# A gated mix of linear attention and a Fourier transform: the hidden transform as seven products of quarters in place of four half products

## The chip, the cores and the metric

The kernel runs on one core of one Trainium2 chip. The metric is the device time of one execution in microseconds (us), the median of several runs; less is better. The core has engines that work side by side, each on its own queue of instructions in order: TensorE (PE, matmuls), VectorE (DVE), ScalarE (ACT), GpSimd (POOL), and SyncE (SP), which here issues most DMA transfers between DRAM and the on-chip memory. They wait for each other by semaphores. Results of matmuls go to eight banks of an accumulator memory.

## The reference

What is computed, cut to its core (S = 2048, D = 576, H = 32 heads of 18 columns, all in 32-bit floats):

```python
q, k, v = qkv[0], qkv[1], qkv[2]             # from x @ wqkv
phi = lambda t: jnp.where(t > 0, t + 1, jnp.exp(t)) + 1e-6
kv = jnp.einsum("bhsd,bhse->bhde", phi(k), v)
a  = num / den @ wo                          # linear attention with phi(q), kv
re = jnp.einsum("bsd,ed->bse", x, dft_hid_re)
im = jnp.einsum("bsd,ed->bse", x, dft_hid_im)
y  = jnp.einsum("ts,bse->bte", dft_seq_re, re) - jnp.einsum("ts,bse->bte", dft_seq_im, im)
g  = sigmoid((x * gate_w).sum(-1, keepdims=True))
out = g * a + (1 - g) * y
```

## The kernel before, in words

Matmuls take operands of a reduced format that keeps the upper bits of a float. Each operand is therefore split: its high part is a copy into that format (`hi_of`, L111, on ScalarE), its low part the rest (`lo_of`, L114, on VectorE), and a full product is three matmuls: high by high, high by low, low by high. Sums ahead of a split are VectorE's (`add`, L117).

S is cut into 16 row tiles of 128, D into four tiles of 128 and a last one of 64, the columns into two halves of 288. The stages, in order:

- K: 16 tiles of x, 28 matmuls each (`k_half`, L266), give phi(k).
- Products over S (L399 to L413, 448 matmuls), from which the per-head matrices come.
- Q: 16 tiles, then products with a matrix M that folds kv and wo into one. Its result, scaled by the gate, is kept in 16 tiles `acc`.
- For the real and then the imaginary part of the transform: a **hidden stage** (`pairs`, L531 to L606) and a **sequence stage** (`sequence`, L645).

The hidden stage takes row tiles in eight pairs (p, p+8). A pair is four products, two tiles by two column halves, of 14 matmuls each (L123): 56. From the four results, VectorE and ScalarE make seven combined factors and split them (`columns` and `rest`). The sequence stage is a product of the 2048x2048 transform with these factors in seven products of quarters instead of eight. It has 32 steps (eight row tiles j of four blocks b); a step uses one matrix block `c` (high and low part) in 42 matmuls (L663). `Matrix.load` (L620) brings a block's 512 KB as `craw`, `Matrix.make` (L629) sums (one 128x512 step and two 128x256), then splits it into two 128x1792 parts. Step n loads block n+3 and makes block n+2. At the end of a row tile, `mix` (L676) adds the result, weighted by the gate, to `acc`; the second sequence stage stores `acc` as the output.

Blocks of `craw` and `c`, the weights and the tiles of x share seven slots of the on-chip memory, laid out by the tables LAY_R and LAY_I. So a block can be loaded only once the reader of what lay there is done. Pairs are counted from 0 to 7. In the program, block 0 is loaded and made after pair 4, block 1 within pairs 6 and 7.

SP's queue follows the program's order up to `in_order.close()` (L759). The order on the other engines, and on SP behind that line, is made by a scheduler that simulates the program. GpSimd has no transfers; it builds masks at the start.

## Time and profile before

| what | us |
|---|---|
| median of 3 runs (lowest, highest) | 745.35 (744.57, 745.51) |
| the profiled execution | 745.01 |
| its span | 743.3 |
| hidden stages in that span, from first to last matmul | 264.43 to 323.79, 502.22 to 561.56 |

In the page, a line such as `L663 PE MATMUL bank<-f,c ... x2688 | 356.9, 295 | 0.0` gives a source line, the engine, the operation, what it writes and reads, the count, the busy time, the mean of one in ns (matmuls overlap, so the mean is longer than the distance of their starts), and the idle time ahead. A row of the timeline gives start, length, engine, line and count, and in brackets the idle time ahead with what ended it. Names in such rows are tiles: `craw` a matrix block as it is summed, `c` its split parts, `f` the factors, `tsum` and `y` the sums at the end of a pair or row tile, `xs` the split tiles of x, `wd` the split weights.

### The profile page before, as it was taken

Reading aid. Unit: us, or ns where it says so; the run is one execution under the profiler, and the core shown is the slowest. Engines: PE = TensorE matmul, PEld = TensorE weight load, DVE = VectorE, ACT = ScalarE, POOL = GpSimd, SP = SyncE. Lnnn points to the kernel's source line nnn. Section 1 sums busy time; section 2 is a strip of 40 time slices with the busy share of each in tenths; the row PEclk is TensorE's granted clock in tenths of the full one; section 3 lists DMA queues with packets and bytes.
Section 4 is the critical chain, followed back from the end, with each engine's and each line's share of the span. In section 5 each row is a group of like instructions: output and inputs, shape, how many; then the busy total and the mean of one; then the engine's idle time right before and its main releaser. Section 6 shows DMA issues by size and latency. Waiting matters only on the chain.

```text
span 743.3 us, 13515 instructions
## 1 busy us (share of the span) xinstructions
PE 735.4 (99%) x5540; PEld 734.1 (99%) x5540; DVE 543.2 (73%) x917; ACT 331.9 (45%) x536; POOL 1.6 (0%) x10
## 2 busy tenths in 40 slices
...
GB/s 168 90 90 158 179 106 145 54 169 72 36 59 92 1 82 89 72 86 115 114 86 88 112 86 86 114 118 117 90 77 113 67 159 130 117 125 139 117 118 33
DMA packets 31715, 75.55 MB, mean 102 GB/s; under 512 B 3301, under 2 KB 9061, under 8 KB 31653
## 3 DMA queue, kind: packets, MB, share of 16 engines
...
q10 hardware_dynamic: 288, 0.41, 0.2%
q14 instruction: 19, 0.15, 0.1%
...
## 4 chain that ended last, share of the span: by engine, by line
PE 99%; DMA 0%; DVE 0%; issue 0%; ACTq 0%; ACT 0%; DVEq 0%
PE bank L663 48%; PE bank L123 41%; PE bank L408 8%; PE bank L719 1%; DMA xraw<-in_xa_dram 0%; PE bank L391 0%; PE bank L394 0%; DVE acc L679 0%; DVE wd L115 0%; DVE xs L285 0%; ACTq L225 0%; ACT L147 0%; DVEq L115 0%; DVE xs L115 0%
## 5 line engine op out<-in xcount | busy, mean ns | idle before, releaser
L663 PE MATMUL bank<-f,c 128*128 128x288 f32 x2688 | 356.9, 295 | 0.0
L663 PEld LDWEIGHTS bank<-f,c 128*128 128x128 f32 x2688 | 356.6, 188 | 0.1
L123 PE MATMUL bank<-wd,xs 128*128 128x288 f32 (+1 forms) x1792 | 243.7, 297 | 4.5 <-DVE xs L115 3.8
L123 PEld LDWEIGHTS bank<-wd,xs 128*128 128x128 f32 x1792 | 240.7, 190 | 5.4 <-ACT wd L112 4.4
L112 ACT ACTIVATE c<-craw 128x1792 fp32r<-128x1792 f32 (+1 forms) x84 | 121.3, 1448 | 225.2 <-DVE craw L118 184.4
L115 DVE TENSOR_TENSOR c<-craw,c 128x1792 fp32r<-128x1792 f32 (+2 forms) x84 | 141.7, 1690 | 37.9 <-ACT c L112 37.7
L118 DVE TENSOR_TENSOR craw<-craw 128x256 f32<-128x256 f32 (+1 forms) x192 | 96.4, 509 | 50.4 <-DMA craw<-in_cr_dram 24.7
L115 DVE TENSOR_TENSOR xs<-xraw,xs 128x640 fp32r<-128x640 f32 (+1 forms) x65 | 52.5, 809 | 17.0 <-ACT xs L112 16.7
L123 PE MATMUL bank<-mw,qs 128*128 128x288 f32 x448 | 63.3, 297 | 0.0
L408 PE MATMUL bank<-pk,c 128*128 128x288 f32 x448 | 60.9, 296 | 0.0
L123 PEld LDWEIGHTS bank<-mw,qs 128*128 128x128 f32 x448 | 60.0, 188 | 0.0
L112 ACT ACTIVATE xs<-xraw 128x640 fp32r<-128x640 f32 x63 | 46.3, 737 | 30.4 <-DMA xraw<-in_xa_dram 30.1
L408 PEld LDWEIGHTS bank<-pk,c 128*128 128x128 f32 x448 | 59.8, 188 | 0.0
L118 DVE TENSOR_TENSOR y<-bank,y 128x288 f32<-128x288 f32 x63 | 28.6, 454 | 10.0 <-PE bank L663 9.3
L258 DVE SCALAR_TENSOR_TENSOR acc<-bank,e 128x288 f32<-128x288 f32 x64 | 27.8, 450 | 10.8 <-ACT e L257 10.7
L256 ACT ACTIVATE e<-bank 128x288 f32<-128x288 f32 x64 | 25.6, 401 | 19.2 <-PE bank L123 19.2
L115 DVE TENSOR_TENSOR f<-tsum,f 128x1152 fp32r<-128x1152 f32 x16 | 21.7, 1356 | 13.3 <-ACT f L112 13.3
L257 ACT ACTIVATE e<-e 128x288 f32<-128x288 f32 x64 | 28.0, 439 | 1.0
L112 ACT ACTIVATE f<-bank 128x288 fp32r<-128x288 f32 x48 | 19.2, 402 | 19.6 <-PE bank L123 11.0
L738 ACT ACTIVATE acc<-bank,gate 128x288 f32<-128x288 f32 x32 | 16.0, 500 | 26.4 <-PE bank L123 26.2
L115 DVE TENSOR_TENSOR f<-bank,f 128x288 fp32r<-128x288 f32 x48 | 21.4, 448 | 8.6 <-ACT f L112 8.6
L112 ACT ACTIVATE f<-tsum 128x1152 fp32r<-128x1152 f32 x16 | 18.6, 1162 | 17.3 <-DVE tsum L118 17.3
...
## 6 DMA issues: line engine op xcount, KB each, us to landing
...
```

What stands on the lines that cost most here:

```text
L112: return nc.scalar.activation(dst, src, AF.Copy, bias=bias)
L115: nc.vector.tensor_tensor(out=dst, in0=src, in1=hi, op=ALU.subtract)
L118: nc.vector.tensor_tensor(out=dst, in0=a, in1=b, op=op)
L123: nc.tensor.matmul(ps, a, b, start=(n == 0), stop=(n == len(pairs) - 1))
L256: nc.scalar.activation(e, ps, AF.Relu, scale=-1.0)
L257: nc.scalar.activation(e, e, AF.Exp, scale=-1.0)
L258: nc.vector.scalar_tensor_tensor(dst, ps, 0.0, e, op0=ALU.max, op1=ALU.add)
L408: nc.tensor.matmul(ps[h][:, :HALF], t[:, a, k], pk[s][:, b, half(h)], start=(s == 0 and n == 0), stop=(s == NT - 1 and n == len(passes) - 1))
L663: nc.tensor.matmul(ps[q], c[x][:, l, k], factors[p][:, y, f], start=(p == 0 and i == 0), stop=(p == NP - 1 and i == 2))
L719: nc.tensor.transpose(banks[c // KC][:, (c % KC) * P:(c % KC + 1) * P], a, ident)
L738: nc.scalar.activation(acc[i][:, half(h)], ps[:, :HALF], AF.Copy, scale=gate[:, i:i + 1])
```

## The change

Over D, x and the hidden weights are cut into quarters: the two halves of D by the two tiles of a pair, and the halves of D by the two column halves. Each half of D has 288 = 2 x 128 + 32 rows. A pair's products become seven products of combined quarters. Each is six matmuls (two tiles of 128 rows, three passes) and one of 96 rows, which holds the three passes of the 32-row rest: 49 matmuls a pair. Results are accumulated in four banks, and the seven factors are sums of them, on VectorE (seven 128x288 sums, a 128x288 split and a 128x1728 split for a pair).

The combined forms are made ahead and kept in DRAM. `Left` makes the forms of x in nine blocks during K and the products over S: a load by GpSimd, four sums of 128x256, a split (128x1792 on both engines), and a store of 1.8 MB by GpSimd. `right` makes the weights' forms in three pieces for each of the two weights, in the Q stage and in the first sequence. The class `Hidden` loads them: seven forms of weights for a stage, seven of x for each pair (262 KB each, into buffers for two pairs: x(p+2,k) follows product k of pair p), and the rest rows (three transfers a pair, runs of 512 bytes). For this, `acc` is no longer kept: GpSimd stores it to DRAM in the Q stage, `sequence` loads its rows as `row` tiles, the first sequence stores the mixed rows as `mid`, and the second loads these. Block 0 is now loaded in pair 6 and made in pair 7; blocks 1 and 2 are loaded in pair 7, and block 1 is made there.

```diff
+PRODUCTS = {1: (4, 0), 6: (2, 4), 2: (6, 1), 5: (1, 3), 7: (0, 5), 3: (3, 2), 4: (5, 6)}
+ORDER = (3, 2, 7, 6, 1, 4, 5)
...
+class Layout:
+    def __init__(self, swap):
+        self.swap = swap
+        a, b = (2, 0) if swap else (0, 2)
+        slot = [SLOT_AT + k * SLOT for k in range(7)]
+        self.low = [slot[a + 1 - swap], WF_AT] + [slot[k] for k in (b + 1 - swap, 4, 6, a + 1 - swap)]
+        self.high = [slot[a + swap], WF_AT + 2 * WF] + [slot[k] for k in (b + swap, 5, a + swap)]
+    def x(self, p, k):
+        h = (p + self.swap) % 2
+        return SLOT_AT + h * 7 * XF + (k if self.swap else 6 - k) * XF
+    def rest(self, p):
+        return WF_AT + 4 * WF if p % 2 else SLOT_AT + 14 * XF + 3 * WF
+    def w(self, k):
+        return WF_AT + k * WF if k < 4 else SLOT_AT + 14 * XF + (6 - k) * WF
...
+    class Left:
+        def __init__(self, k, start, after):
+            self.c = at(start, [P, 7, 2, 2 * P], R, "xb")
+            self.f = self.c.bitcast(F)
+            self.k = k
+            begin_after(nc.gpsimd.dma_start(out=self.f[:, 3:7, 1], in_=xq[k]), after)
+        def make(self):
+            r, c = self.f[:, :, 1], self.c
+            add(r[:, 0], r[:, 4], r[:, 3], ALU.subtract)
+            add(r[:, 1], r[:, 5], r[:, 3])
+            add(r[:, 2], r[:, 1], r[:, 4], ALU.subtract)
+            add(r[:, 3], r[:, 6], r[:, 2], ALU.subtract)
+            hi_of(c[:, :, 0], r)
+            lo_of(c[:, :, 1], r, c[:, :, 0])
+            nc.gpsimd.dma_start(out=xforms[self.k], in_=self.f)
+    def right(src, rest, start):
+        main, last = scratch([P, 7, 2, 2, HALF], "wm"), scratch([96, 7, HALF], "wm")
+        def pieces():
+            for k in range(3):
+                n = P if k < 2 else 96
+                c = at(start, [P, 7, 2, HALF], R, "wb")[:n]
+                f = c.bitcast(F)
+                r = f[:, :, 1]
+                if k < 2:
+                    nc.gpsimd.dma_start(out=r[:, 0:3], in_=src[k, :, 0:3])
+                    nc.gpsimd.dma_start(out=r[:, 5], in_=src[k, :, 3])
+                else:
+                    for j in range(3):
+                        rows = slice(32 * j, 32 * j + 32)
+                        nc.gpsimd.dma_start(out=r[rows, 0:3], in_=rest[:, 0:3])
+                        nc.gpsimd.dma_start(out=r[rows, 5], in_=rest[:, 3])
+                yield
+                add(r[:, 3], r[:, 5], r[:, 0], ALU.subtract)
+                add(r[:, 5], r[:, 2], r[:, 5], ALU.subtract)
+                add(r[:, 4], r[:, 2], r[:, 3], ALU.subtract)
+                add(r[:, 6], r[:, 4], r[:, 1], ALU.subtract)
+                hi_of(c[:, :, 0], r)
+                if k < 2:
+                    lo_of(c[:, :, 1], r, c[:, :, 0])
+                    nc.gpsimd.dma_start(out=main[:, :, k], in_=f)
...
+        if i % 3 == 2 and i // 3 < 4:
+            left = Left(i // 3, SLOT_AT + 15104 + i // 3 % 2 * 14336, done[-1])
+        if i % 3 == 1:
+            left.make()
...
-            if step in (4, 5):
-                wqt.load(step - 4)
-            if step >= 8:
+            for k, (a, o) in enumerate(((0, SLOT_AT + 15104), (3, SLOT_AT + 29440), (6, ACC_AT),
+                                        (10, ACC_AT), (13, ACC_AT + 14336))):
+                if step == a:
+                    left = Left(4 + k, o, done[-1])
+                if step == a + 2:
+                    left.make()
+            if step in (8, 9):
+                wqt.load(step - 8)
+            if step >= 11:
...
+        if i in (5, 7, 9):
+            next(wr_pieces, None)
...
-            if p == NP - 4:
-                m.load(0)
-                m.make(0)
...
+    class Hidden:
+        def __init__(self, weights, lay):
+            (self.main, self.last), self.lay = weights, lay
+            self.w, self.x, self.rest = {}, {}, {}
+        def load_w(self, k):
+            f, o = PRODUCTS[ORDER[k]][1], self.lay.w(k)
+            wl, rl = at(o, [P, 4, HALF], R, "wf"), at(o + 4 * HALF * 4, [P, HALF], R, "wf")
+            wm, rm = wl.bitcast(F), rl.bitcast(F)
+            nc.sync.dma_start(out=wm.rearrange("p (c s) n -> p c s n", c=2), in_=self.main[:, f])
+            nc.sync.dma_start(out=rm[:96], in_=self.last[:, f])
+            self.w[k] = wl, rl
+        def load_rest(self, p):
+            g, row = p // 4, p % 4 * 32
+            self.rest[p] = at(self.lay.rest(p), [P, 7, P], R, "xr")
+            r = self.rest[p].bitcast(F)
+            for j in range(3):
+                nc.sync.dma_start(out=r[32 * j:32 * j + 32],
+                                  in_=xforms[NP][row:row + 32, :, j // 2, g * P:g * P + P])
+        def load_x(self, p, k):
+            o = self.lay.x(p, k)
+            self.x[p, k] = at(o, [P, 4, P], R, "xf")
+            r = self.x[p, k].bitcast(F)
+            nc.sync.dma_start(out=r.rearrange("p (s c) n -> p s (c n)", s=2),
+                              in_=xforms[p][:, PRODUCTS[ORDER[k]][0]])
+        def product(self, ps, p, k, start):
+            x, (w, wl) = self.x[p, k], self.w[k]
+            ops = [(x[:, a * 2 + c], w[:, 2 * c + b]) for c in range(2) for a, b in FULL]
+            ops.append((self.rest[p][:96, PRODUCTS[ORDER[k]][0]], wl[:96]))
+            for n, (a, b) in enumerate(ops):
+                nc.tensor.matmul(ps, a, b, start=(start and n == 0), stop=(n == len(ops) - 1),
+                                 skip_group_check=True)
+        def run(self, m):
+            for p in range(NP):
+                hi = at(T_AT + p * TPAIR, [P, 7, HALF], R, "fh")
+                o = T_AT + p * TPAIR + 7 * HALF * 4
+                t, lo = (at(o, [P, 7, HALF], d, "fl") for d in (F, R))
+                p3, p2, e = (at(y_ring.next(), [P, HALF], F, "y") for _ in range(3))
+                be, bx, bg, bf = (bank()[:, :HALF] for _ in range(4))
+                for k, q in enumerate(ORDER):
+                    ps = {3: be, 6: be, 5: be, 2: bx, 1: bx, 7: bg, 4: bf}[q]
+                    self.product(ps, p, k, q in (3, 2, 7, 4))
+                    if p + 2 < NP:
+                        self.load_x(p + 2, k)
+                    if p == NP - 2 and k == 3:
+                        m.load(0)
+                    if p == NP - 1 and k == 0:
+                        m.make(0)
+                    if p == NP - 1 and k == 1:
+                        m.load(1)
+                    if p == NP - 1 and k == 4:
+                        m.load(2)
+                        m.make(1)
+                    if q == 3:
+                        nc.scalar.activation(p3, be, AF.Copy)
+                    elif q == 2:
+                        nc.scalar.activation(p2, bx, AF.Copy)
+                    elif q == 7:
+                        add(t[:, 5], bg, p3, ALU.subtract)
+                    elif q == 6:
+                        add(e, be, p2, ALU.subtract)
+                    elif q == 1:
+                        hi_of(hi[:, 0], bx)
+                        add(t[:, 4], bx, t[:, 5])
+                        lo_of(lo[:, 0], bx, hi[:, 0])
+                    elif q == 4:
+                        add(t[:, 6], bf, e, ALU.subtract)
+                        add(t[:, 1], t[:, 4], t[:, 6], ALU.subtract)
+                    else:
+                        add(t[:, 3], be, p2, ALU.subtract)
+                        add(t[:, 2], t[:, 3], t[:, 4])
+                if p + 2 < NP:
+                    self.load_rest(p + 2)
+                hi_of(hi[:, 1:], t[:, 1:])
+                lo_of(lo[:, 1:], t[:, 1:], hi[:, 1:])
+                factors.append((hi, lo))
...
-                o = self.low.next()
+                n, low = self.loaded, self.lay.low
+                o = low[n] if n < 2 else low[2 + (n - 2) % 4]
...
+                row = {t: at(mix_ring.next(), [P, D], F, "row") for t in (j, j + NP)}
+                for t, a in row.items():
+                    nc.sync.dma_start(out=a, in_=src[t])
...
+                    nc.sync.dma_start(out=dst[t][:, cs], in_=a)
...
+        nc.gpsimd.dma_start(out=att[i], in_=acc[i])
+        if i == 1:
+            next(wr_pieces, None)
+        if 6 <= i < 9:
+            hidden.load_w(i - 2)
+        if i >= 9:
+            hidden.load_x(0, i - 9)
+            hidden.load_x(1, i - 9)
+        for k, j in enumerate((9, 10, 12, 14)):
+            if i == j:
+                hidden.load_w(k)
+        if i == 10:
+            hidden.load_rest(0)
+    hidden.load_rest(1)
...
     def late(n):
+        if n in (4, 8, 12, 16):
+            next(wi_pieces, None)
+        if n == 20:
+            for k in range(4):
+                second.load_w(k)
         if n == NP * NB - 3:
+            second.load_rest(0)
+            for k in range(3):
+                second.load_x(0, k)
         if n == NP * NB - 2:
-    pairs(wdr, mr)
-    sequence(mr, gate_n, between=late)
+            for k in range(3, 7):
+                second.load_x(0, k)
+            second.load_w(4)
+        if n == NP * NB - 1:
+            second.load_w(5)
+            second.load_w(6)
+            second.load_rest(1)
+            for k in range(7):
+                second.load_x(1, k)
+    first.run(mr)
+    sequence(mr, gate_n, att, mid, between=late)
     factors.clear()
-    pairs(wdi, mi)
-    sequence(mi, gate_m, last=gate_n)
+    second.run(mi)
+    sequence(mi, gate_m, mid, [out[t * P:(t + 1) * P] for t in range(NT)], last=gate_n)
```

**VectorE at the first handover.** Before, block 0 (`craw_3754`, `c_3760`) stands among the steps of the first pair; `f` and `tsum` are that pair's factors:

```order
L115 TENSOR_TENSOR f_3399<-bank,f_3399 128x288
L118 TENSOR_TENSOR craw_3754<-craw_3754 128x512
L118 TENSOR_TENSOR craw_3754<-craw_3754 128x256 x2
L115 TENSOR_TENSOR f_3399<-bank,f_3399 128x288
L115 TENSOR_TENSOR c_3760<-craw_3754,c_3759 128x1792
L118 TENSOR_TENSOR tsum_3404<-tsum_3404,bank 128x288
L118 TENSOR_TENSOR tsum_3404<-bank,tsum_3404 128x288
L115 TENSOR_TENSOR xs_3375<-xraw_3376,xs_3375 128x640
```

After, these rows stand at the end of the stage. `craw_4115`, `craw_4180`, `craw_4206` and `craw_4300` are blocks 0, 1, 2 and 4, `c_4169` is the low part of block 0, `fl_4076` the wide split of pair 6, `fl_4149` and `fl_4150` are steps of pair 7, of which the last before `c_4169` needs the last hidden product; ahead of the first row stands the 128x512 sum of `craw_4180`:

```order
L159 TENSOR_TENSOR craw_4115<-craw_4115 128x256
L159 TENSOR_TENSOR fl_4149<-bank,fl_4149 128x288
L159 TENSOR_TENSOR craw_4206<-craw_4206 128x512
L159 TENSOR_TENSOR craw_4180<-craw_4180 128x256
L156 TENSOR_TENSOR fl_4150<-bank,fh_4148 128x288
L156 TENSOR_TENSOR fl_4076<-fl_4075,fh_4074 128x1728
L159 TENSOR_TENSOR craw_4300<-craw_4300 128x512
L159 TENSOR_TENSOR craw_4206<-craw_4206 128x256
L159 TENSOR_TENSOR craw_4180<-craw_4180 128x256
L159 TENSOR_TENSOR fl_4149<-bank,y_4153 128x288
L159 TENSOR_TENSOR fl_4149<-bank,y_4152 128x288
L156 TENSOR_TENSOR c_4169<-craw_4115,c_4168 128x1792
```

The low part of block 0 has moved from the first pair to a place behind the sums of blocks 1, 2 and 4 and the steps of pair 7.

**TensorE at the same place.** Before, the last product of a pair is followed by the sequence with both parts of block 0 (`c_3759` high, `c_3760` low):

```order
L123 MATMUL bank<-wd_2876,xs_3848 128x288 x2
L123 MATMUL bank<-wd_2877,xs_3848 128x288
L123 MATMUL bank<-wd_2876,xs_3848 128x288 x3
L663 MATMUL bank<-f_3399,c_3759 128x288 x2
L663 MATMUL bank<-f_3399,c_3760 128x288
L663 MATMUL bank<-f_3484,c_3759 128x288 x2
L663 MATMUL bank<-f_3484,c_3760 128x288
```

After, the end of pair 7 (`xf_40..` its forms, `xr_4068` its rest rows, `wf_..` the weights' forms and, one number on, their rest) and the start of the sequence, with `fh` and `fl` the factors' parts and `c_4168` the high part of block 0:

```order
L697 MATMUL bank<-wf_3193,xr_4068 128x288
L697 MATMUL bank<-wf_3249,xr_4068 128x288
L697 MATMUL bank<-wf_3361,xr_4068 128x288
L697 MATMUL bank<-wf_3074,xr_4068 128x288
L697 MATMUL bank<-wf_3468,xf_4031 128x288 x6
L697 MATMUL bank<-wf_3469,xr_4068 128x288
L697 MATMUL bank<-wf_3021,xf_4041 128x288 x6
L697 MATMUL bank<-wf_3022,xr_4068 128x288
L697 MATMUL bank<-wf_3136,xf_4064 128x288 x6
L697 MATMUL bank<-wf_3137,xr_4068 128x288
L803 MATMUL bank<-fh_3534,c_4168 128x288
L803 MATMUL bank<-fl_3536,c_4168 128x288
```

The rest products of pair 7 with the first four forms stand apart from their main products, and the first 14 matmuls of the sequence use the high part alone; the low part `c_4169` follows in the 15th.

**GpSimd in the K stage.** Before, its queue has no transfers. After, its queue holds the loads of `Left` (`xb`) and the stores of the forms (`xm`):

```order
L317 DMA xb_312<-in_xq_dram 128x4x256
L327 DMA xm_94<-xb_312 128x3584
L317 DMA xb_456<-in_xq_dram 128x4x256
L317 DMA xb_600<-in_xq_dram 128x4x256
L327 DMA xm_95<-xb_456 128x3584
L327 DMA xm_96<-xb_600 128x3584
L317 DMA xb_744<-in_xq_dram 128x4x256
L317 DMA xb_992<-in_xq_dram 128x4x256
L327 DMA xm_97<-xb_744 128x3584
L317 DMA xb_1096<-in_xq_dram 128x4x256
L327 DMA xm_98<-xb_992 128x3584
```

A store waits for the split of its block, and the loads behind it stand in the same queue.

182 lines of the change are left out of this document (74 added, 108 removed).

## The prediction

> **What bounds the kernel now.** I began with the first and fourth parts of the page and the list of what TensorE waits for.
>
> ```profile
> span 743.3 us, 13515 instructions
> PE 735.4 (99%) x5540; PEld 734.1 (99%) x5540; DVE 543.2 (73%) x917; ACT 331.9 (45%) x536; POOL 1.6 (0%) x10
> DMA packets 31715, 75.55 MB, mean 102 GB/s; under 512 B 3301, under 2 KB 9061, under 8 KB 31653
> PE 99%; DMA 0%; DVE 0%; issue 0%; ACTq 0%; ACT 0%; DVEq 0%
> PE bank L663 48%; PE bank L123 41%; PE bank L408 8%; PE bank L719 1%; DMA xraw<-in_xa_dram 0%; PE bank L391 0%; PE bank L394 0%; DVE acc L679 0%; DVE wd L115 0%; DVE xs L285 0%; ACTq L225 0%; ACT L147 0%; DVEq L115 0%; DVE xs L115 0%
> ```
> ```profile
> PE bank L123 <- DVE xs L115: 3.8, 1, 3.8
> PE bank L123 <- DVE wd L115: 0.4, 1, 0.4
> PE bank L123 <- DVE xs L285: 0.2, 1, 0.2
> ```
>
> The reader sees a kernel that is a row of matmuls and nothing else: TensorE is busy for 99% of the span, the chain of waits is TensorE from end to end, and all its waits together are 4.4 us, at the start. So a matmul removed is time removed, as long as no new wait appears. Every wait that the change makes is paid in full, since no idle time of TensorE is there to take it.
>
> Next came the stages. The windows view, cut at the first matmuls of each stage (start to end, length, then busy time and count of each engine), and the timeline of TensorE at the two places where a hidden stage hands over to a sequence stage (start, length, instructions):
>
> ```profile
> 264.43:323.79 59.36, 59.36 (x450) 59.36 (x449) 41.32 (x76) 29.58 (x51) 0.00 (x0) 1.00 0.29 85
> 323.79:502.22 178.43, 178.43 (x1347) 178.29 (x1345) 142.11 (x202) 62.07 (x50) 0.00 (x0) 1.00 0.31 101
> 502.22:561.56 59.34, 59.34 (x451) 59.34 (x450) 45.93 (x83) 30.12 (x52) 0.00 (x0) 1.00 0.31 94
> ```
> ```profile
> 323.79 28.40 PE L663 MATMUL bank<-f,c 128*128 128x288 f32 x212
> ...
> 561.56 8.63 PE L663 MATMUL bank<-f,c 128*128 128x288 f32 x64
> ```
>
> Each hidden stage is 448 matmuls in 59.36 and 59.34 us, 0.1325 us each, at a granted clock of 1.00. Neither handover has an idle bracket: the sequence starts at once. The next rows say why. They are VectorE's at 269 us, some 50 us ahead of the first sequence matmul:
>
> ```profile
> 269.02 1.61 DVE L118 TENSOR_TENSOR craw<-craw 128x512 f32<-128x512 f32 x3 [1.63 <-DMA craw<-in_cr_dram]
> ...
> 272.45 2.02 DVE L115 TENSOR_TENSOR c<-craw,c 128x1792 fp32r<-128x1792 f32 x1 [1.45 <-ACT c L112]
> 274.39 0.45 DVE L118 TENSOR_TENSOR tsum<-tsum,bank 128x288 f32<-128x288 f32 x1
> ```
>
> The first matrix block is loaded, summed and split early in the stage, so nothing is due at its end.
>
> **The gain.** Seven matmuls for eight on the same 128x288 shape: 56 to 49 a pair, 8 pairs, two stages, 112 removed, 112 x 0.1325 = 14.84 us. The seven rest matmuls of a pair have 96 rows instead of 128; I take them at the same price, since the columns that stream are the same.
>
> **The first handover.** The change loads block 0 in pair 6 and makes it in pair 7, and loads blocks 1 to 4 as the stage's buffers come free. The price of this is VectorE's queue at the end of the stage, which the order above shows. Its steps are priced from these rows (the spacing of starts is what a queued step costs):
>
> ```profile
> L115 DVE TENSOR_TENSOR c<-craw,c 128x1792 fp32r<-128x1792 f32 x64 | 129.1, 2020 | 15.5 <-ACT c L112 15.5
> ```
> ```profile
> 368.61 0.33 SPq L625 DMA_DIRECT2D craw<-in_cr_dram  x1
> ...
> 369.18 0.44 DVE L118 TENSOR_TENSOR y<-y,bank 128x288 f32<-128x288 f32 x1
> 369.54 0.41 DVE L118 TENSOR_TENSOR craw<-craw 128x256 f32<-128x256 f32 x1
> 369.88 0.45 DVE L118 TENSOR_TENSOR y<-bank,y 128x288 f32<-128x288 f32 x1
> ...
> 371.86 0.69 DVE L118 TENSOR_TENSOR craw<-craw 128x512 f32<-128x512 f32 x1 [0.47 <-DMA craw<-in_cr_dram]
> 372.47 0.45 DVE L118 TENSOR_TENSOR y<-bank,y 128x288 f32<-128x288 f32 x1
> ```
>
> A 128x288 step costs 0.36 us, 128x256 0.34, 128x512 0.61, and 128x1792 1.94 (272.45 to 274.39); 128x1728 is then 1.87. A block's load takes 371.86 - 368.61 = 3.25 us from issue to the step that waited for it.
>
> Let E be the end of the last hidden matmul. By the new order of TensorE, block 1's buffer (the first two weight forms) has its last reader 23 matmuls before E, at E-3.05, so it lands at E+0.2; block 2 is issued behind it, and with 0.5 MB at the 385 GB/s quoted below it lands 1.4 us later, at E+1.6; block 4's buffer (under the form of the fifth product) is free at E-1.86. VectorE, in order, from E+0.2: block 1's first sum 0.61, 0.34, a step of pair 7 0.36, to E+1.5; block 2's from its landing, 0.61, 0.34, 0.36, to E+2.9; the wide split of pair 6 1.87, E+4.8; block 4's sum 0.61, then 0.34, 0.34, 0.36, 0.36, E+6.8; at last the low part of block 0, 1.94, E+8.8. TensorE has 14 sequence matmuls that use block 0's high part only, 1.86 us. It then waits 8.8 - 1.86 = 6.9 us, taken as **7.0**. Lower end: all blocks have landed in time, and and only the steps behind pair 7's fifth product (E-1.86) count: 0.36+0.61+0.34+0.36+1.87+0.61+0.34+0.34+0.36+0.36+1.94 = 7.5, so E+5.6 and a wait of 3.8. Upper end: loads collide with pair loads and land 2.5 us later, 9.5.
>
> **The second handover.** The same queue, with other neighbours. Block 1's buffer is free 30 matmuls before E, lands at E-0.7, and the low part of block 0 stands behind ten steps: 0.61+0.34+0.36+0.36+0.36+0.61+0.34+0.36+0.61+0.34 and 1.94 are 6.2, so E+5.5 and a wait of 3.7 us as the lower end. One of the ten frees the bank into which pair 7's last product accumulates, and with it that product waits as well, inside the same 3.7. Blocks 2 and 4 land up to 1.5 us late as before, 0.8 taken, and the low part of block 1 comes about 7 us after block 0's, where one step of the sequence (42 x 0.1325 = 5.6 us) gives less cover: 1.5 us more. I take **6.0**, from 3.7 to 8.
>
> **Between first sequence and second hidden stage.** Four quarters of pair 1 and two weight forms lie under the last sequence buffers and can only be issued once these are read: 2.3 MB, 0.33 us an issue, 3.25 us to land. The sixth product of pair 0 is due 35 matmuls (4.6 us) after the start. I take **1.5 us**, between 0 (all in time) and 6 (the forms land last at 385 GB/s).
>
> **The hidden stages' transfers.** A pair needs 7 x 262 KB and 344 KB of rest rows, 2.18 MB in 6.49 us, 336 GB/s, where before moved 85 (row above). What the trace has at its busiest, by windows (last three numbers: clock, share of the DMA engines, GB/s):
>
> ```profile
> 3.00:9.00 6.00, 4.53 (x15) 3.68 (x16) 4.57 (x11) 3.60 (x8) 0.00 (x0) 1.00 1.01 356
> 62.00:66.00 4.00, 4.00 (x32) 4.00 (x32) 2.55 (x4) 2.49 (x7) 0.00 (x0) 1.00 0.96 319
> 86.00:91.00 5.00, 5.00 (x42) 5.00 (x41) 4.42 (x7) 2.00 (x4) 0.00 (x0) 1.00 1.00 324
> 221.00:226.00 5.00, 5.00 (x40) 5.00 (x40) 4.09 (x13) 3.77 (x9) 0.00 (x0) 1.00 1.06 385
> ```
>
> Six pairs are loaded within a stage, 13.1 MB: 41 us at 319 GB/s, due at about 51. Buffers for two pairs hide that. The second stage has 2.3 MB more, 48 us at 319. So nothing is late by itself, but little is spare: **1.0 us** for both, from 0 to 5 (280 GB/s, 55 us in the second).
>
> **K, S and Q stages.** Here VectorE and ScalarE also prepare the forms: nine blocks of x, each 4 x 0.34 + 1.94 = 3.3 us of VectorE and one 128x1792 copy on ScalarE, and six pieces of weights, each 4 x 0.36 + 2.2 = 3.6.
>
> ```profile
> 20.00:30.00 10.00, 10.00 (x78) 10.00 (x77) 6.95 (x13) 8.27 (x18) 0.00 (x0) 1.00 0.34 98
> ...
> 50.00:60.00 10.00, 10.00 (x78) 10.00 (x77) 5.89 (x11) 7.50 (x16) 0.00 (x0) 1.00 0.32 96
> ...
> 170.00:180.00 10.00, 10.00 (x79) 10.00 (x78) 10.00 (x21) 9.15 (x22) 0.00 (x0) 1.00 0.30 78
> ```
> ```profile
> L112 ACT ACTIVATE c<-craw 128x1792 fp32r<-128x1792 f32 x64 | 108.7, 1704 | 193.8 <-DVE craw L118 184.4 <-PE bank L663 8.9
> ```
>
> Three K tiles are 84 matmuls, 11.1 us. VectorE is busy 59 to 70% of it, 6.5 to 7.7, and 3.3 more make 9.8 to 11.0; ScalarE's 75 to 83% and 1.7 make 10.0 to 10.9. It just fits, and the matmuls cover it. In the Q stage VectorE has no gap between 170 and 180 us, but 18% between 221 and 226, and 36 us of the first sequence, are free for the pieces. What can break the cover is a wait in VectorE's queue for a load that GpSimd issues, or SP's: the load of wq stands behind the stores of forms. I take **2.0**, between 0 and 10.
>
> GpSimd issues 59 transfers, and no row of before shows one. The nearest row is SP's: 0.33 us to issue, 3.25 to land, and I price them so. The Trainium skill ("SBUF — State Buffer", section "SBUF: two separate sides", in its box on the DVE blocking DMA) says that such transfers starve of descriptors while VectorE holds the port that it shares with GpSimd, and gives 620 ns alone against about 3100 beside such an operation; by that, an estimate of 2.5 us more for each of the nine loads of x, 22 us, would be the upper price if nothing covered it. No run here shows it.
>
> **Sum.** The profiled execution took 745.01 us, its span and 1.7 around it. 745.01 - 14.84 + 7.0 + 6.0 + 1.5 + 1.0 + 2.0 = 747.67; the median of the runs lies 0.34 above that execution, so **748.0**. A measurement tells 0.2% from no change, 743.9 to 746.8.
>
> **Rivals.**
> - *The gain outlasts the handovers* (0.30). Blocks land in time, both waits are at their lower ends, 3.8 and 3.7, and the rest is covered: 745.35 - 14.84 + 7.5 = 738.0. For it: VectorE has 30% of a hidden stage free (41.32 of 59.36) to run ahead. Against it: the queue's order puts three blocks' sums ahead of block 0's low part.
> - *GpSimd's transfers come late* (0.13). VectorE takes its queue in order, and in K has about 1 us of slack in 11. Each of nine loads that lands more than 1 us late stops feature maps behind it, and TensorE with them; at 2 us late, 9 us in all, 757 us. It decides from 1 us on. For it: VectorE's share of 59 to 70%; against: the loads stand two tiles ahead.
> - *The transfers bound the hidden stages* (0.07). Below 13.1 MB in 50 us, 262 GB/s, the first stage waits, below 300 the second: at 250, 2 and 10 us, 760. For it: rest rows of 512 bytes. Against: 319 at the least in the four windows.
> - *No handover wait at all* (0.05): the order on the chip hides both, 730.5.
>
> My forecast, between 744 and 752 for most of it, has 0.45. The range is 736 to 760; outside lie the last rival and the ends of the others. Faster: 0.30 + 0.05 = 0.35. Same: a third of the forecast, 0.15. Slower: 0.30 + 0.13 + 0.07 = 0.50.
>
> **What would show it.** Right: 112 matmuls fewer at the same 0.1325 us; a wait of TensorE for the low part of a matrix block on VectorE, 5 to 9 us, about 14 matmuls after each hidden stage; no other wait over 2 us. Wrong: sequences that start without idle time (rival one); waits spread over the K stage with VectorE idle on GpSimd's loads (rival two); TensorE waiting for x forms in pairs 3 to 7 (rival three). If the rest matmuls cost less than 0.1325 us, the gain is larger than said.

## The result, and the profile after

The changed kernel takes **786.56 us**, median of 4 runs (782.39 to 791.52), beside 745.43 (744.57 to 745.86) of the kernel before: a ratio of 1.0556, with an interval of 1.049 to 1.0622. The prediction was 748.0, with a range of 736 to 760. It is slower, as forecast, but by 41 us where 2.6 were forecast.

The first and fourth parts of the page of after:

```profile
span 783.1 us, 13886 instructions
PE 739.8 (94%) x5428; PEld 729.2 (93%) x5428; DVE 580.3 (74%) x966; ACT 329.1 (42%) x493; POOL 39.6 (5%) x70
DMA packets 69798, 159.98 MB, mean 204 GB/s; under 512 B 7396, under 2 KB 22692, under 8 KB 68580
PE 60%; DMA 22%; DVE 9%; issue 5%; ACT 1%; SPq 1%; POOL 0%; DVEq 0%; ACTq 0%; POOLq 0%
```

The 112 matmuls are gone (5540 to 5428), and yet TensorE is busy for 4.4 us **more** (739.8 for 735.4). At 0.1325 us apiece, 112 fewer should make 720.6. So 39.8 us of longer span are made of three things: −14.84 for the matmuls, 34.7 of new waits (TensorE waits 39.2 us in all, 4.5 before), and 19.2 of matmuls that take longer than before; 0.7 is left over. The chain of waits was TensorE alone; now 22% of it are transfers and 9% VectorE.

The windows view cuts these by stage: span up to the first hidden matmul, hidden, sequence, hidden, sequence (start to end, length, then busy time and count of PE, PEld, DVE, ACT, POOL; clock, share of the DMA engines, GB/s). The first two rows are the first and the last stage of the kernel before, the others are after:

```profile
0.00:264.43 264.43, 259.96 (x1956) 258.99 (x1957) 173.01 (x355) 152.68 (x343) 1.60 (x10) 1.00 0.33 100
561.56:739.91 178.35, 178.35 (x1346) 178.12 (x1344) 140.33 (x201) 57.47 (x43) 0.00 (x0) 1.00 0.33 112
```
```profile
0.00:279.68 279.68, 264.12 (x1957) 260.81 (x1957) 204.84 (x405) 165.57 (x345) 30.46 (x56) 0.99 0.67 231
279.68:340.92 61.24, 53.97 (x394) 52.16 (x392) 39.27 (x72) 22.30 (x33) 0.54 (x1) 1.00 0.88 280
340.92:527.57 186.65, 182.55 (x1344) 181.11 (x1345) 150.99 (x213) 62.47 (x43) 8.63 (x13) 0.98 0.59 194
527.57:597.08 69.51, 58.86 (x395) 55.57 (x393) 41.44 (x76) 20.31 (x32) 0.00 (x0) 0.95 0.96 273
597.08:779.48 182.40, 180.33 (x1346) 179.52 (x1344) 143.26 (x203) 58.46 (x41) 0.00 (x0) 0.99 0.37 125
```

Every stage is longer than before: by 15.25, 1.88, 8.22, 10.17 and 4.05 us. Length less busy time is the waiting: 15.6, 7.3, 4.1, 10.7, 2.1. The hidden stages have 56 matmuls fewer each, 7.42 us, and are longer nevertheless. The rows below group TensorE's waits by what ended them (us, times, longest):

```profile
PE bank L697 <- DMA xr<-xm: 9.7, 8, 2.2
PE bank L803 <- DVE c L156: 5.3, 5, 1.8
PE bank L169 <- DVE xs L156: 5.0, 3, 3.9
PE bank L697 <- DVE y L159: 4.2, 2, 2.6
PE bank L517 <- ACT c L153: 3.3, 2, 1.7
PE bank L169 <- ACT xs L153: 3.0, 2, 2.1
PE bank L169 <- ACT kvb L153: 2.2, 1, 2.2
...
PE bank L697 <- DMA xf<-xm: 1.0, 3, 0.6
```

The largest group is `xr`, the rest rows (L697 is a hidden product). L169 and L517 lie ahead of the hidden stage, L803 is a sequence. In all they are 33 waits.

The first handover, in the timeline of TensorE (start, length, count; in brackets the idle time ahead and what ended it):

```profile
338.00 1.05 PE L697 MATMUL bank<-wf,xf 128*128 128x288 f32 x6 [1.67 <-DVE y L159]
338.89 0.30 PE L697 MATMUL bank<-wf,xr 96*128 96x288 f32 x1
340.92 0.40 PE L803 MATMUL bank<-fh,c 128*128 128x288 f32 x1 [1.73 <-ACT c L153]
...
341.36 0.44 PE L803 MATMUL bank<-fh,c 128*128 128x288 f32 x1
341.60 0.44 PE L803 MATMUL bank<-fl,c 128*128 128x288 f32 x1
...
344.86 0.40 PE L803 MATMUL bank<-fh,c 128*128 128x288 f32 x1 [0.90 <-DVE fl L159]
...
347.16 0.54 PE L803 MATMUL bank<-fh,c 128*128 128x288 f32 x2 [1.76 <-DVE c L156]
```
```profile
342.00:344.00 2.00, 1.96 (x9) 1.62 (x7) 2.00 (x3) 0.00 (x0) 0.00 (x0) 0.50 0.78 173
...
350.00:352.00 2.00, 2.00 (x12) 2.00 (x12) 2.00 (x4) 1.69 (x2) 0.00 (x0) 0.64 0.00 0
...
354.00:356.00 2.00, 2.00 (x17) 2.00 (x17) 2.00 (x2) 1.91 (x2) 0.00 (x0) 1.00 0.59 236
```

Two things are to be seen. The wait for block 0 is there, but cut up: 1.67 for a bank ahead of the last hidden product, 1.73 for the high part, 0.90 for a factor, 1.76 for the low part, 6.06 us in all, close to the 7.0 forecast. Only the last of the four is the wait that the prediction described.

And after the first two waits, matmuls start 0.24 us apart for 0.13: between 342 and 344 us the granted clock is 0.50. Between 346 and 348 us it is 1.00 again, behind the next two waits it falls a second time (0.51 between 348 and 350), and from 352 us on it stays at 1.00. The Trainium skill ("TensorE: Matmul & The Clock Gate", section "HAM oscillation — how this bites in real kernels") asks for no idle gaps over about 3.4 us; here two gaps of 1.67 and 1.73 us, 1.2 us of matmuls apart, were enough. No limit follows from them: a like pair at 71 us, 1.52 and 1.55 us with 0.8 us of matmuls between, left the clock at 1.00 (73 to 78 us), and so did a wait of 2.20 us at 157.

By the windows view the clock of after is at about half in six stretches of 3.4 us, from 180.8, 341.2, 348.0, 559.7, 583.6 and 597.2 us on. Half speed over these 20.5 us is worth at most 10 of the 19.2 us of longer busy time. Some 5 more are in how busy time is counted: the last matmul ahead of a wait counts with its whole 0.30 us (338.89 above), where the next one otherwise starts after 0.13, and there are 30 more waits than before. Both are estimates; 4 us or more stay open.

### The profile page after: what moved, and what is told of

Same layout as the page of the kernel before. It is cut to its first block, busy times and chain, and to the rows that moved or that the text cites. A ratio compares the mean times of both kernels' runs of the same rounds, so it can differ in the third digit from the quotient of the medians.

```text
span 783.1 us, 13886 instructions
## 1 busy us (share of the span) xinstructions
PE 739.8 (94%) x5428; PEld 729.2 (93%) x5428; DVE 580.3 (74%) x966; ACT 329.1 (42%) x493; POOL 39.6 (5%) x70
## 4 chain that ended last, share of the span: by engine, by line
PE 60%; DMA 22%; DVE 9%; issue 5%; ACT 1%; SPq 1%; POOL 0%; DVEq 0%; ACTq 0%; POOLq 0%
PE bank L803 33%; PE bank L169 16%; DMA xr<-xm 6%; PE bank L697 6%; PE bank L517 4%; DMA xb<-in_xq_dram 3%; DMA wm<-wb 3%; DVE c L156 2%; DMA xraw<-in_xa_dram 2%; DMA xf<-xm 2%; DMA craw<-in_xg_dram 1%; DMA wb<-in_wi_dram 1%; DVE craw L159 1%; DMA craw<-in_cr_dram 1%; PE bank L859 1%
## 5 line engine op out<-in xcount | busy, mean ns | idle before, releaser
L803 PE MATMUL bank<-fh,c 128*128 128x288 f32 x1792 | 361.4, 298 | 7.9 <-DVE c L156 5.3
L803 PEld LDWEIGHTS bank<-fh,c 128*128 128x128 f32 x1792 | 289.9, 190 | 10.2 <-DVE c L156 6.8
L803 PE MATMUL bank<-fl,c 128*128 128x288 f32 x896 | 264.1, 298 | 0.0
L803 PEld LDWEIGHTS bank<-fl,c 128*128 128x128 f32 x896 | 170.9, 191 | 0.0
L169 PE MATMUL bank<-wd,xs 128*128 128x288 f32 (+1 forms) x896 | 128.0, 303 | 8.5 <-DVE xs L156 5.0
L169 PEld LDWEIGHTS bank<-wd,xs 128*128 128x128 f32 x896 | 123.7, 193 | 10.9 <-ACT wd L153 4.1
L697 PE MATMUL bank<-wf,xf 128*128 128x288 f32 x672 | 103.8, 303 | 6.5 <-DVE y L159 4.2
L697 PEld LDWEIGHTS bank<-wf,xf 128*128 128x128 f32 x672 | 95.8, 194 | 9.6 <-DVE y L159 4.7
L517 PE MATMUL bank<-pk,c 128*128 128x288 f32 x448 | 62.0, 297 | 4.8 <-ACT c L153 3.3
L517 PEld LDWEIGHTS bank<-pk,c 128*128 128x128 f32 x448 | 60.1, 189 | 5.6 <-ACT c L153 3.6
L169 PE MATMUL bank<-mw,qs 128*128 128x288 f32 x448 | 63.2, 297 | 0.0
L169 PEld LDWEIGHTS bank<-mw,qs 128*128 128x128 f32 x448 | 59.9, 188 | 0.0
L156 DVE TENSOR_TENSOR fl<-fl,fh 128x1728 fp32r<-128x1728 f32 x16 | 31.3, 1955 | 12.2 <-ACT fh L153 12.0
L159 DVE TENSOR_TENSOR ys<-bank,ys 128x288 f32<-128x288 f32 x63 | 28.5, 453 | 14.5 <-PE bank L803 13.7
L697 PE MATMUL bank<-wf,xr 96*128 96x288 f32 x112 | 27.6, 307 | 9.7 <-DMA xr<-xm 9.7
```

The lines of the kernel that those rows point to most:

```text
L156: nc.vector.tensor_tensor(out=dst, in0=src, in1=hi, op=ALU.subtract)
L159: nc.vector.tensor_tensor(out=dst, in0=a, in1=b, op=op)
L169: nc.tensor.matmul(ps, a, b, start=(n == 0), stop=(n == len(pairs) - 1))
L517: nc.tensor.matmul(ps[h][:, :HALF], t[:, a, k], pk[s][:, b, half(h)], start=(s == 0 and n == 0), stop=(s == NT - 1 and n == len(passes) - 1))
L697: nc.tensor.matmul(ps, a, b, start=(start and n == 0), stop=(n == len(ops) - 1), skip_group_check=True)
L803: nc.tensor.matmul(ps[q], c[x][:, l, k], factors[p][y][:, f], start=(p == 0 and i == 0), stop=(p == NP - 1 and i == 2))
```

## The experiments

Two theories for the largest part, at first: **one**, TensorE waits for rest rows in the hidden stages and for VectorE, which waits for transfers, elsewhere; **two**, it is the bytes (160 MB for 76) that slow everything.

### The rest rows

`rest_once`, `load_rest`: pairs 2 to 7 use the rest rows of pairs 0 and 1.

```diff
+            if p >= 2:
+                self.rest[p] = self.rest[p % 2]
+                return
```

> The rest rows are loaded for pairs 0 and 1 only; pairs 2 to 7 use those of the pair two before, so their results are others. Theory 1 (the short runs of the rest rows, 512 bytes from 32 rows, fill the DMA engines in the hidden stages): the 9.7 us of waits for xr go, with them the slow stretches of TensorE behind them, and the two hidden stages, 59.5 and 69.7 us in the changed kernel, come near 52 to 54 and 54 to 57: 764 to 772 us in all. Theory 2 (the bytes as such bind: 2.18 MB a pair): 16% of the bytes go, the second stage falls by 3 to 6 us only, waits move from xr to xf, 779 to 783 us. Theory 3 (the loads are late by SP's queue, not by the engines): waits for xf instead, no more than 2 us gained.

Measured 767.1 us, ratio 1.0284 (1.0254 to 1.0314): 19 us of the 41 are gone. The two hidden stages:

```profile
283.05:339.12 56.07, 53.53 (x395) 53.09 (x394) 39.74 (x73) 20.98 (x33) 0.54 (x1) 0.98 0.80 256
525.70:580.25 54.55, 51.83 (x387) 51.25 (x385) 39.69 (x74) 20.43 (x31) 0.00 (x0) 1.00 0.88 305
```

The second falls from 69.51 to 54.55 while moving more per second (305 GB/s for 273). So the stage was not short of bandwidth as such, but of one small transfer. In after, windows while the rest rows come in show why:

```profile
562.00:565.00 3.00, 3.00 (x21) 3.00 (x21) 0.79 (x2) 0.41 (x1) 0.00 (x0) 0.82 1.15 214
571.00:574.00 3.00, 3.00 (x23) 2.83 (x23) 2.66 (x7) 0.41 (x1) 0.00 (x0) 1.00 1.16 200
```

The DMA engines are as busy as they get (1.15) at 214 GB/s, where the prediction's row had 1.06 at 385: 512-byte runs fill the engines with few bytes. Over this stage the trace's packets of 512 bytes took 48 ns each, those of 2048 bytes 107. And the rest rows are asked for late:

```profile
575.77 1.85 SPq L682 DMA_DIRECT2D xr<-xm  x3
...
583.09 0.91 PE L697 MATMUL bank<-wf,xr 96*128 96x288 f32 x4 [2.17 <-DMA xr<-xm]
```

The last of these three landed at 582.95 us by the trace, 7.2 us behind the first issue, and a pair takes 6.49. Which of the two, length of runs or lead? Three kernels: `rest_packed` stores the rest rows per pair, so that a pair's come as one transfer of 3584-byte runs; `rest_four` gives them four buffers and asks for them a pair earlier; `rest_four_packed` does both.

```diff
...
-            for j in range(3):
-                nc.sync.dma_start(out=r[32 * j:32 * j + 32],
-                                  in_=xforms[NP][row:row + 32, :, j // 2, g * P:g * P + P])
+            nc.sync.dma_start(out=r[:96], in_=xrest[p])
```
```diff
-        return WF_AT + 4 * WF if p % 2 else SLOT_AT + 14 * XF + 3 * WF
+        return (SLOT_AT + 14 * XF + 3 * WF, WF_AT + 4 * WF, MIX_AT, MIX_AT + XR)[p % 4]
...
+                        if k == 0:
+                            self.load_rest(p + 2)
```

> The rest rows are laid out pair by pair when they are stored (24 small stores by GpSimd at the end of the products over S), and a pair's rest comes in one transfer of 96 rows of 3584 bytes. The bytes stay the same. Theory 1 (short runs): the hidden stages gain nearly what they gain without the loads, 5 to 15 us. Theory 2 (bytes): under 2 us. In both, the stages ahead of the hidden one may lose 0 to 4 us by the 24 stores.

> The rest rows get four buffers in place of two (in the memory of the row tiles, unused in a hidden stage), and those of pair p+2 are loaded ahead of its x forms, at the start of pair p, not at its end. Bytes and runs stay. Theory A (a rest row has one pair of time, 6.5 us, to land and cannot): the waits for xr, 3.8 us in the first and 6.0 in the second hidden stage, go, and 8 to 15 us with the slow matmuls. Theory B (the DMA engines are full: share 0.88 and 0.96 in the two stages): waits move from xr to xf, no more than 3 us gained.

> Both at once: rest rows stored pair by pair and loaded in one transfer with long runs, four buffers, two pairs of time. Theory A and the short runs together: hidden stages of 53 to 57 us up to their last product, no wait for xr or xf over 0.5 us in the first, 768 to 776 us in all. Theory B (bytes): the second hidden stage stays over 62 us.

Measured 785.27 us (1.0528, 1.0397 to 1.0658), 780.05 (1.0472, 1.0363 to 1.0581) and **769.47** (1.033, 1.0248 to 1.0412). By the totals, long runs alone give nothing that can be told from after, four buffers alone little, and both together 17 us. But the totals also hold the stretch ahead of the hidden stage, whose length is not steady (below): it took 279.68 us in after and 292.11 in `rest_four`, with the same code there. The hidden stages themselves, of `rest_packed`, `rest_four` and `rest_four_packed`:

```profile
280.85:341.52 60.67, 54.01 (x387) 52.70 (x385) 37.94 (x71) 20.80 (x33) 0.54 (x1) 0.96 0.92 287
531.43:594.81 63.38, 56.57 (x394) 53.32 (x393) 42.03 (x78) 21.15 (x32) 0.00 (x0) 0.99 0.92 300
```
```profile
292.11:351.44 59.33, 53.52 (x394) 53.08 (x393) 39.73 (x73) 20.98 (x33) 0.54 (x1) 0.96 0.93 287
536.93:596.08 59.15, 54.82 (x394) 53.69 (x393) 42.15 (x74) 22.17 (x32) 0.00 (x0) 0.97 1.01 314
```
```profile
283.24:334.81 51.57, 51.48 (x388) 51.26 (x386) 34.35 (x62) 20.09 (x31) 0.54 (x1) 1.00 1.00 309
522.10:578.68 56.58, 53.31 (x394) 52.25 (x392) 41.80 (x74) 22.09 (x32) 0.00 (x0) 1.00 1.01 319
```

Both stages together are 130.75 us in after, then 124.05, 118.48 and 108.15, and the waits for rest rows are 9.7, 4.4, 0.7 and none. So lead alone takes away nearly all of these waits, and the length of the runs alone about half. In the third kernel the first hidden stage is without a wait: 51.57 for the 59.36 of before, 7.8 us, the whole gain of 56 matmuls (7.42). This is the fastest version that computes everything, and it is still slower than before.

### Bytes or VectorE in the K stage

`forms_short` stores and loads two of the seven forms of x; VectorE does all as in after.

```diff
+            n = 2 if self.k < NP else 7
+            nc.gpsimd.dma_start(out=xforms[self.k][:, :n], in_=self.f[:, :n])
...
```

> Of each block's seven forms of x only two are stored (0.5 MB for 1.8), and the pairs load these two in place of all seven; the results are others. Sums, splits, the order of loads and all issues stay. Theory A (bytes: K, products over S and Q move some 47 MB in 160 us, near what the DMA engines have, and the loads of x and xg that feed TensorE come late): the first hidden stage starts at 268 to 272 us instead of 279.7 (264.4 before the change). Theory B (GpSimd's transfers start late, whatever their size, and VectorE's queue waits for them): 277 to 280. Theory C (VectorE's and ScalarE's added work): 277 to 280 as well. The hidden stages change little.

Measured 792.46 us (1.0624, 1.058 to 1.0667). The stages ahead of the hidden one take 287.8 us, no less than after's 279.7, so fewer bytes alone don't shorten this stretch. They move its waits: none of TensorE's falls between 8 and 67 us any more, where after has 0.89 and 0.36, and more come from 70 us on. Theory two fell as the main cause. `left_one` makes one of the nine blocks of x and uses its forms for all:

```diff
-        if i % 3 == 2 and i // 3 < 4:
+        if i == 2:
...
-                                  in_=xforms[NP][row:row + 32, :, j // 2, g * P:g * P + P])
+                                  in_=xforms[0][row:row + 32, :, j // 2, g * P:g * P + P])
```

> Of the nine blocks of x forms only the first is made; all pairs load that one's forms (results are others). The weights' forms, the stores of the attention result, the hidden stages and their transfers stay. Theory: the blocks (their loads, sums, splits and stores together, on VectorE, ScalarE and the DMA engines) make the 11 us of waits ahead of the hidden stage and the slow matmuls behind them: the first hidden stage then starts at 265 to 271 us (264.4 before the change, 279.7 to 290.9 with all nine). Rival: the weights' pieces and the moved load of wq make most of it: 275 us or later.

Measured 772.62 us (1.0368, 1.0338 to 1.0398). The same stretch:

```profile
0.00:270.58 270.58, 260.30 (x1956) 258.49 (x1957) 180.02 (x365) 152.63 (x337) 19.87 (x40) 1.00 0.53 170
```

270.6 us: eight blocks cost at least 9 us here, and about 6 of the 15 remain for the weights' pieces and what else is new. `left_light` keeps nine loads, nine stores and ScalarE's copies (of four forms), and takes VectorE's sums and low parts out:

```diff
...
-            lo_of(c[:, :, 1], r, c[:, :, 0])
-            nc.gpsimd.dma_start(out=xforms[self.k], in_=self.f)
+            hi_of(c[:, 3:7, 0], r[:, 3:7])
+            nc.gpsimd.dma_start(out=xforms[self.k][:, 3:7], in_=self.f[:, 3:7])
```

> Nine blocks as in the change, but without VectorE's work: no sums and no low parts, ScalarE splits four forms of seven, and four of seven are stored (1.05 MB a block for 1.8); results are others. forms_short, with all the work and 0.5 MB a block, had no wait of TensorE in the K stage between 8 and 70 us, but 10 us of waits from 71 on, and started the hidden stage at 287.8. Theory A (VectorE's added work makes the waits from 71 us on): the first hidden stage starts at 266 to 273 us. Theory B (loads of GpSimd's that VectorE does not wait for also delay others by the bytes): 276 or later, with waits of 1 us and more for ScalarE's splits behind loads of x and xg.

Measured 783.24 us (1.0515, 1.0457 to 1.0572), with the rest rows' waits as before; the stretch ahead of the hidden stage:

```profile
0.00:272.98 272.98, 262.31 (x1957) 260.65 (x1958) 176.71 (x360) 158.19 (x345) 30.40 (x56) 0.99 0.65 212
```

About the same as with one block. The length of this stretch is not steady: kernels that run the same code there had 279.68 (after), 283.05 (`rest_once`), 290.87 (`handover`, below), 292.11 (`rest_four`) and 295.86 us (`handover_two`, below). The 287.8 of `forms_short` lies among these, and both 270.6 and 273.0 lie below the lowest. So it is VectorE's part in the blocks that costs, its work or its waits for their loads, more than their bytes. ScalarE is not quite ruled out, since `left_light` also copies four forms of seven. How a wait in the K stage comes about shows in the timeline of after:

```profile
37.24 0.78 POOL L317 DMA_DIRECT2D xb<-in_xq_dram  x1 [2.05 <-ACT e L302]
44.87 0.76 DVE L159 TENSOR_TENSOR xb<-xb 128x256 f32<-128x256 f32 x2 [2.02 <-DMA xb<-in_xq_dram]
45.24 0.74 ACT L153 ACTIVATE xs<-xraw 128x640 fp32r<-128x640 f32 x1 [0.91 <-DMA xraw<-in_xa_dram]
46.03 1.73 PE L169 MATMUL bank<-wd,xs 128*128 128x288 f32 x8 [0.89 <-ACT xs L153]
```

The load needs 7.6 us from issue to the step that waited for it, not 3.25: the 1.8 MB store of block 0 went out ahead of it on GpSimd's queue at 34.65 us. VectorE idles 2.02 us for it, in order. But TensorE's wait of 0.89 us ends on ScalarE, and that waited for a tile of x that SP loads. By the trace this load was issued at 37.73 us and landed 7.5 us later; before, the same load left at 37.71 and took 3.0. Between 36 and 40 us the DMA engines are full (1.05 and 1.08, at 442 and 423 GB/s). So with stores of 1.8 MB the loads of x come late as well; with the 0.5 MB of `forms_short` this one took 4.5 us, and TensorE did not wait. There the other way is seen: VectorE idles 2.93 us at 66.44 for a load of GpSimd's, and TensorE's wait of 2.93 us at 70.97 ends on VectorE. Two edits tried to take the cause apart. `lead` makes each block a tile later and the first weights' piece earlier:

```diff
-        if i % 3 == 1:
-            left.make()
+            if i > 2:
+                left.make()
```

> Each block of x forms in the K stage is summed three tiles after its load is issued, not two, and the first piece of weights is loaded two Q tiles earlier. Theory (VectorE takes its queue in order and waits there for loads that GpSimd issued, which land 5 to 8 us after issue; TensorE waits behind it): the waits near 46 and 48 us and near 157 us go, 3 to 4 us, and the waits of VectorE for xb and wb (2.0 us at 44.9 and at 155.4) with them; the others, near 71, 123 and 179, stay. Rival (VectorE's and ScalarE's work as such is too much): the waits only move to other tiles and their sum stays near 11 us.

Measured 790.58 us (1.0609, 1.0529 to 1.0689). It tells nothing: the scheduler put the sums back where they were, and VectorE still waited for the load (2.82 us at 46.27). `left_pool` takes `rest_four_packed` and moves the sums and low parts of the x blocks from VectorE to GpSimd.

```diff
-            add(r[:, 0], r[:, 4], r[:, 3], ALU.subtract)
+            pool(r[:, 0], r[:, 4], r[:, 3], ALU.subtract)
...
-            lo_of(c[:, :, 1], r, c[:, :, 0])
+            pool(c[:, :, 1], r, c[:, :, 0], ALU.subtract)
```

> rest_four_packed with the sums and low parts of the x blocks on GpSimd in place of VectorE, nothing left out. left_light, without VectorE's share of these blocks, began the hidden stage at 273.0 us; the kernels with it at 279.7 to 295.9. Theory (VectorE's added work ahead of the hidden stage, not GpSimd's transfers as such, makes most of the loss there): the first hidden stage starts at 268 to 276 us and the kernel takes 752 to 764 us, for 769.5 in rest_four_packed. Rival (GpSimd is too slow for a block in 11 us, or holds VectorE up while it works): 280 us or later, 770 or more.

Measured 813.16 us (1.091, 1.0878 to 1.0942): the rival held. From 20 to 62 us, the low part of a tile of x on VectorE (count, busy, mean ns, idle ahead), with GpSimd's own steps, and then the same in after:

```profile
L156 DVE TENSOR_TENSOR xs<-xraw,xs 128x640 fp32r<-128x640 f32 x10 | 12.7, 1268 | 6.5 <-ACT xs L153 6.4
...
L324 POOL TENSOR_TENSOR xb<-xb 128x1792 fp32r<-128x1792 f32 x2 | 8.1, 4027 | 3.8 <-ACT xb L153 3.8
L324 POOL TENSOR_TENSOR xb<-xb 128x256 f32<-128x256 f32 x10 | 9.5, 964 | 12.5 <-DMA xb<-in_xq_dram 12.2
```
```profile
L156 DVE TENSOR_TENSOR xs<-xraw,xs 128x640 fp32r<-128x640 f32 x11 | 8.9, 820 | 1.5 <-ACT xs L153 1.5
```

The first hidden stage began at 310.73 us, 27 us later than in `rest_four_packed`. VectorE's step went from 820 to 1268 ns. The Trainium skill ("SBUF — State Buffer", section "Who interferes with whom") says that a VectorE instruction with two inputs in that memory contends with a GpSimd instruction that reads it; these rows agree.

### The handovers

`handover` lets the sums of blocks 1 to 6 wait for the low part of the block before, and moves the wide splits of pairs 6 and 7 behind the low parts of blocks 0 and 1. `handover_two` lets the sums, and both wide splits, wait for block 0's parts alone.

```diff
+                if self.last is not None and self.made < 7:
+                    tc.add_manual_dep(first.ins, self.last.ins.name, mybir.DependencyInfo(
...
+            if pend:
+                pend.pop(0)(after=m.splits[n])
```

> Only the order at the two handovers is changed: block 0's low part ahead of the sums of later blocks (each block's sums follow the low part of the one before), and the wide splits of pairs 6 and 7 behind blocks 0 and 1. Theory: VectorE's queue makes the waits there, and each wait is paid again by TensorE's slower clock behind it. Then from the last hidden matmul to steady sequence (some 8.3 us lost at the first, 5 to 7 at the second, with 3 to 4 us more of slow matmuls each) 12 to 18 us go, 766 to 774 us in all. Rival: the blocks land late, because the hidden stage's transfers are late, and the order of the queue changes nothing: 780 to 786.

> As in handover, but a block's sums follow only the low part of block 0, not that of the block before it. The first version moved the loss: 2.4 us of waits at the first handover in place of 6.1, but 11 us more in the next eight steps, where each block's sums stood behind the low part of the one before. Theory A (that chain of VectorE and ScalarE steps made the later waits): both handovers together lose 3 to 6 us of waits, none over 1 us in later steps. Theory B (VectorE has more to do behind the handover than fits, in any order: five blocks, two wide splits and the steps of pair 7 at once): waits of 5 us or more come again within some eight steps, whatever stands first.

Measured 803.96 us (1.0778, 1.0638 to 1.0918) and 796.62 (1.069, 1.0561 to 1.0819): no gain either time. In `handover` only 1.55 and 0.88 us of waits are left at the first handover, but each of the next steps waits 0.9 to 1.84 for its block; in `handover_two` the wait is one of 5.95 us. The windows of `handover` behind the handover, and its waits:

```profile
351.71:401.60 49.89, 38.95 (x269) 35.88 (x269) 40.06 (x55) 20.58 (x13) 3.63 (x5) 1.00 0.50 163
```
```profile
PE bank L822 <- ACT c L153: 16.1, 13, 2.1
```

In `handover` VectorE is idle for 10 of these 50 us: the order that the edit forces, each block's sums behind the low part before, makes the waits. In `handover_two` VectorE is busy without a gap from 356 to 376 us, as it is in after from 340 to 358, so its work there does not fit into the time. Neither of the two orders helped; in both, each sequence is also longer than in after (195.86 and 190.89 us for 186.65 in the first).

`before_late` prices a wait by itself. It is the kernel before, complete, with block 0 made only behind the last pair's wide split; no forms, no new transfers.

```diff
-                m.make(0)
...
+        m.after = self_last[0]
+        m.make(1)
```

> The kernel before, with one edit: at the two handovers block 0 is made only after the last pair's wide split, so that TensorE must wait there, with no other part of the change in it. Theory (a wait costs its length and then slow matmuls: the granted clock falls to about half for some microseconds behind a wait of about 2 us or more): TensorE waits some 4 to 7 us at each handover and the kernel loses more than it waits, by 2 to 5 us a handover, with spacings of 0.24 us in place of 0.13 behind the waits: 757 to 768 us. Rival: the time lost equals the waits to within 1 us a handover.

Measured 780.39 us (1.0472, 1.0438 to 1.0507). The waits were larger than expected, 14.73 and 15.38 us, and the span 34.6 us longer, 4.5 more than the waits.

```profile
PE bank L669 <- ACT c L112: 30.1, 2, 15.4
```
```profile
339.46 5.74 PE L669 MATMUL bank<-f,c 128*128 128x288 f32 x31 [14.73 <-ACT c L112]
```

The first 31 matmuls behind it take 5.74 us, where 31 x 0.1325 are 4.1. The two sequences, busy from end to end, are 1.35 and 2.0 us longer than before. So a wait of this length costs 1.4 to 2 us of slow matmuls besides.

### Everything off at once

`all_off` is `left_one` and `rest_once` together, with blocks 0 to 3 of each matrix neither loaded nor made. `all_off_weights` also makes only one of the six pieces of weights.

```diff
+                if self.loaded < 4:
+                    self.raws.append(None)
...
-            for k in range(3):
+            for k in range(1):
```

> Of the changed kernel three things are left out, so that its results are others: eight of the nine blocks of x forms, the rest rows of pairs 2 to 7, and blocks 0 to 3 of both sequences, which use factors in their place, so that nothing has to be made at the handovers. The 112 matmuls stay away, the weights' pieces and all other transfers stay. Theory (the loss is the sum of three causes, each with its slow matmuls: blocks ahead of the hidden stage, rest rows in it, handovers behind it): 733 to 742 us, faster than before, the 14.8 us of the removed matmuls less 6 us that the weights' pieces cost ahead of the hidden stage (270.6 in left_one against 264.4). Rival (something else, such as the store and reload of the attention result or the 96-row matmuls, takes the gain): 746 us or more.

> all_off with one piece of weights' forms in place of six (both stages load that piece's forms; results are others). Theory (the pieces made in the Q stage and in the first sequence are what is left of the loss: the hidden stage began 5.8 us late in all_off, and its first sequence had 4.4 us of waits): 731 to 738 us, that is the gain of 14.8 us but for what a load or two still costs. Rival (the gain of the removed matmuls itself is smaller, or the stores and reloads of the attention result cost the rest): 741 us or more.

Measured 744.17 us (0.9985, 0.9974 to 0.9996), above what was expected, and 737.84 (0.9905, 0.9875 to 0.9935). The first row is `all_off` from the first hidden matmul on; then `all_off_weights`, ahead of it and from it on:

```profile
270.27:743.70 473.43, 464.05 (x3474) 461.86 (x3472) 349.90 (x529) 149.48 (x140) 9.08 (x14) 1.00 0.55 183
```
```profile
0.00:269.13 269.13, 261.72 (x1956) 260.56 (x1957) 173.50 (x355) 150.52 (x335) 13.53 (x30) 0.99 0.49 156
269.13:735.00 465.87, 461.48 (x3474) 460.60 (x3472) 339.51 (x514) 145.02 (x137) 0.54 (x1) 1.00 0.53 172
```

Before, that second part took 743.3 − 264.43 = 478.9 us. `all_off` has 473.4, with 4.4 us of waits behind the weights' pieces in the first sequence; without those pieces it is 465.9, 13.0 of the 14.84 us. The matmuls are worth what the prediction gave them, and four kinds of side work eat it: rest rows, blocks of x, weights' pieces, blocks at the handover. The first stretch is still 4.7 us longer than before, of which one wait of 2.7 us for `kvb`.

## Why the prediction was right or wrong

- **The gain, 14.84: right.** The first hidden stage of `rest_four_packed` has it in full, and `all_off_weights` 13.0 for both.
- **The handovers, 7.0 and 6.0: near in size, the cause right in part.** 6.06 us at the first; 2.57, 0.96 and 1.10, 4.63, at the second, plus 1.0 for other steps of that stage (`y`, `fl`). VectorE's queue was priced well: the low part of block 0 was done 7.9 us behind the last hidden matmul, for the 8.8 forecast. But the sign of being right, a wait of 5 to 9 us for the low part behind each hidden stage, did not come: that wait is 1.76 and 0.96 us. The rest are waits ahead of the last hidden product (1.67 and 2.57), for a factor (0.90), for a later block's low part (1.10), and for the high part of block 0 (1.73), which ScalarE split behind pair 6's wide split; the prediction had no queue of ScalarE there.
- **Between first sequence and second hidden stage, 1.5: near in size, by luck in part**, 1.0 (the `xf` row). The sixth product of pair 0, which was expected to wait, did not; these waits come 12.9 to 18.3 us into the stage, in pairs 1 and 2.
- **The hidden stages' transfers, 1.0: wrong.** The `xr` row has 9.7. The step that failed is "Six pairs are loaded within a stage, 13.1 MB: 41 us at 319 GB/s" with "Buffers for two pairs hide that". It took the rate of long runs for runs of 512 bytes (214 GB/s at a full share), and for the rest rows two buffers mean a lead of one pair, since a buffer is read until its pair's last product. Four buffers alone left 0.7 us of these waits, long runs alone 4.4, both together none; so the lead is the larger part. Rival three had the place and the doubt ("rest rows of 512 bytes"), with a chance of 0.07.
- **K, S and Q stages, 2.0: wrong.** 10.9 us of new waits. The step was "It just fits, and the matmuls cover it": busy time was added up against 11.1 us per three tiles, with loads at 3.25 us, though VectorE takes its queue in order and loads took up to 7.6 us with the added stores in the DMA engines. Rival two had half of this mechanism, GpSimd's loads; that SP's loads of x come late too stood in no rival. Removing eight blocks gave at least 9 us. The 22 us that the prediction estimated from the Trainium skill ("SBUF — State Buffer", section "SBUF: two separate sides") did not appear as such: the new waits are half of that, and the one followed above came with the DMA engines full. Whether the waits for loads or the work itself costs more stays open, since `left_light` took both away and `lead` did not move the sums. The 1.4 us that are left in the first sequence belong to weights' pieces or blocks. (GpSimd issues 60 transfers, not 59, which changes nothing.)
- **Matmuls at 0.1325 us throughout: wrong, 19.2 us.** Each wait was priced at its length alone. `before_late` shows 1.4 to 2 us behind one long wait, and after has some 30 new waits, shorter ones: 34.7 us of waits and 19.2 of slower matmuls, on average 1.8 us for each wait together. Half of the 19.2 is the clock at most, and only some of the waits brought it down.

These terms sum to it: −14.84 + 6.06 + 4.63 + 1.0 + 1.0 + 9.7 + 10.9 + 1.4 + 19.2 = 39.1, of the 39.8 between the spans. Two rivals that were held apart happened in part, both at once, together with the forecast's own waits, and the clock made some of them dearer.

Not tried: moving the forms to 240 to 280 us of after, where VectorE is busy for less than 10 of 40 us. Why the first stretch varies by 16 us in like kernels (279.68 to 295.86) is not settled.
